# Second product of hidden groups 1 and 2 of the first MLP as seven block products, and all four W2 tiles of group 3 split behind them

## The chip, the cores and the metric

One Trainium2 chip, one of its cores. The kernel is a single program; its engines are TensorE (PE, with its weight loads shown apart as PEld), VectorE (DVE), ScalarE (ACT), GpSimd (POOL) and SyncE (SP), which issues nearly all DMAs. The metric is the device time of one execution in microseconds (us); the number given for a kernel is the median of several executions. A profile is one further execution, and its span runs from its first instruction to its last.

## What is computed

The reference, cut to what matters here (x has 2304 rows and 512 columns, each MLP has 2048 hidden features):

```python
kv  = np.einsum('bhsd,bhse->bhde', k, v)
out = np.einsum('bhsd,bhde->bhse', q, kv)
x   = out / rms(out) * g_norm          # regrouped to 2304 tokens x 512
h = x @ w_in                           # first MLP
x = softplus(h) @ w_out
h = x @ w_in2                          # second MLP
return leaky_relu(h, 0.01) @ w_out2
```

Each MLP is thus a first product (x @ w_in), a function of each element, and a second product (g @ w_out). The change touches second products of the first MLP alone.

## The kernel before, in words

**Numbers.** Every float32 operand of a matmul is held as two parts, a rounded one (ACT copies it, "high") and the rest (DVE subtracts, "low"). One product of two 128-deep tiles is therefore three matmuls: high by high, high by low, low by high.

**Tiles.** The hidden features of an MLP are cut into four groups of 512; groups 0 to 3 belong to the first MLP, 4 to 7 to the second. The 2304 tokens are cut into three pairs of two blocks of 384 (`BN`). One round of the main loop, a *pair* `t`, is one group and one pair of token blocks, so the MLPs are 24 pairs, three to a group. A pair has two steps `s` = 2t and 2t+1, each for half of the group's features (two tiles of 128). x, and what the second products add up to, lie in the tensor `xy`.

**First product, all groups.** Each step makes its 2 by 2 by 2 blocks with seven block products instead of eight (`product`, L819), from sums and differences of x blocks that are written to the DRAM scratch `xscr` once and loaded again for each pair (L802). `after` collects the results from PSUM (copies on ACT L1086, additions on DVE L1093) and applies the function.

**Second product, two ways.** In the plain way (`quarter`, L1135 for the first MLP, L1151 for the second) the eight combinations of feature half, token block and output half are made in four quarters of 24 matmuls, 96 matmuls of 384 columns for a pair; the results are added to `xy` by eight DVE additions (`to_xy`, L709). Its left operands are four W2 tiles that `split_w2` cuts into high and low (ACT L628, DVE L634). Its right operands are four hidden blocks that `parts` cuts into high and low (ACT L848, DVE L853). In the block way (`second`, L1046), used before in groups 5, 6 and 7, seven block products are made for a pair: `g_part` forms sums and differences of the hidden blocks (four DVE subtractions, L928) and splits seven of them (L848, L853); `w2_part` does the same with the W2 blocks once per group (four DVE operations L964, seven splits L978 and L981); `piece` i, j runs six matmuls, and `to_y` (L1025) adds what the PSUM bank holds to `xy` after each block product, fourteen additions for a pair. The second product of a pair is run one pair later, between the block products of the next first product.

**Weights.** W1 and W2 come as 64-bit numbers; `decode_w` loads a tile into one of two raw buffers (SP, L580 and L585) and builds float32 from it (ACT L594, DVE L600, L606, L612).

**Order.** The code records operations with their reads and writes; `Plan.run` then fixes the order on each engine ahead of time from a table of its own costs. On the chip every engine takes its list strictly in that order, and semaphores hold an instruction until what it reads is there and what it overwrites has been read.

**Buffers.** `rb` holds the split hidden blocks and W2 tiles, `rc` (once the attention is over) saved x blocks and decoded W2 tiles, `mf` hidden blocks and raw weights. The PSUM banks 0 to 3 serve the first product, 4 to 7 the second.

Of the kernel before, what the change touches and what calls it, by code (L numbers as in the profile page):

```python
# [131 lines left out]
def linear_attention_two_mlps(  # L132
# [154 lines left out]

    wx = [Reg("ra", at * KI, [2, 256]) for at in (18, 20)]

    gB = [Reg("rb", 6 * i * KI, [2, 2, BN]) for i in range(2)]  # L290
    gA = [Reg("rb", (12 + 6 * i) * KI, [2, 2, BN]) for i in range(3)]
    cB = Reg("mf", 20 * KI, [2, BN])
    cA = [Reg("mf", at * KI, [2, BN]) for at in (17, 4)]
    dram = ctx.enter_context(tc.tile_pool(name="dram", bufs=1, space=bass.MemoryType.DRAM))
    xscr = dram.tile([NTP * 7 + 1, P, 4 * BN], F32, name="xscr")

    SG = (NG + 1, NG + 2, NG + 3)
    cS = [Reg(n, at * KI, [2, BN]) for n, at in (("mf", 4), ("mf", 17), ("mf", 20), ("mf", 11), ("mf", 14), ("rc", 0))]
    gS = [Reg("rb", 6 * i * KI, [2, 2, BN]) for i in range(4)]
    wS = {j: Reg("rb", at * KI, [2, 2, 256]) for j, at in zip((1, 4, 5, 6, 3, 2, 0), (38, 42, 46, 50, 30, 34, 26))}  # L300
    fS = [[Reg("rc", (3 + 4 * u + 2 * m) * KI, [DM], I32) for m in range(2)] for u in range(2)]
    fT = Reg("rc", 11 * KI, [2, 256])

# [313 lines left out]
    def decode_pair(F, which, i):  # L617

        for m in range(2):
            decode_w(F + m, which, half[i][m])  # L620

    def split_w2(F, i):
        for m in range(2):
            d_, w_ = half[i][m], w2s[(F + m) % NW2]
            hk, lk = w_.keys(0, 4 * DM), w_.keys(4 * DM)
            op(
                {"A": t_a(DM)},
                lambda e, d_=d_, w_=w_: nc.scalar.activation(  # L628
                    w_[:, 0, :], d_.ap.bitcast(F32), AF.Copy
                ), d_.keys(), hk,  # L630
            )
            op(
                {"D": t_d(DM)},
                lambda e, d_=d_, w_=w_: ENG[e].tensor_tensor(  # L634
                    w_[:, 1, :], d_.ap.bitcast(F32), w_[:, 0, :].bitcast(F32), ALU.subtract
                ), d_.keys() + hk, lk,
            )

# [217 lines left out]

    FIRST = {(0, 0): 0, (1, 0): 1, (0, 1): 5, (1, 1): 6}

    def first_blocks():
# [15 lines left out]
            )  # L879

    def plain(s, k_):
        c, g_ = (cB, gB[s % 2]) if k_ else (cA[s % 2], gA[s % 3])
        w_ = wst[s % 2]
        for m in range(2):
            o = ps[2 + m][:, :BN]
            for j in range(2):

                e_, W_, part_ = xe[FIRST[j, k_]], *((wx[s], 0) if m + j == 0 else (w_, 2 * m + j - 1))

                def fn(e, j=j, o=o, e_=e_, W_=W_, part_=part_):  # L890
# [13 lines left out]
                op({"PE": 6 * t_mm[BN]}, fn, wk + e_.keys(), [("ps", 2 + m)])
            from_psum(c[:, m, :], o, BN, 2 + m, c.keys(4 * BN * m, 4 * BN * (m + 1)))
        act(s, lambda: c.ap, lambda: c.ap, 2 * BN, c.keys(), c.keys())
        parts(c, g_)

    def in_S(t):
        return t // NTP in SG  # L910

    S_pairs = [t for t in range(2 * NG * NTP) if in_S(t)]

    def block(t, u, k_):
        return cS[(4 * S_pairs.index(t) + 2 * u + k_) % len(cS)]

    def c_of(s):
        if in_S(s // 2):
            return block(s // 2, s % 2, 0), block(s // 2, s % 2, 1)
        return cA[s % 2], cB  # L920

    def g_part(t, i):
        b = {(u, k_): block(t, u, k_) for u in range(2) for k_ in range(2)}

        def minus(to, x, y):
            op(
                {"D": t_d(2 * BN)},
                lambda e: nc.vector.tensor_tensor(to.ap, x.ap, y.ap, ALU.subtract),  # L928
                x.keys() + y.keys(), to.keys(),
            )  # L930

        if i == 1:
            minus(b[0, 0], b[0, 1], b[0, 0])
        elif i == 2:
            minus(b[0, 0], b[1, 1], b[0, 0])
        elif i == 4:
            minus(b[0, 1], b[1, 1], b[0, 1])
        elif i == 6:
            minus(b[1, 0], b[1, 0], b[0, 0])
        src = b[((0, 0), (0, 0), (0, 0), (1, 1), (0, 1), (1, 0), (1, 0))[i]]  # L940
        parts(src, gS[(7 * S_pairs.index(t) + i) % len(gS)])

    def w2_decode(g, u):
        for m in range(2):
            decode_w(GF * g + 2 * u + m, 1, fS[u][m])

    def w2_part(i):


        def blk(a, u):  # L950
            at = (3 + 4 * u) * KI // 4
            ap = bufs["rc"][:, at:at + 2 * DM].rearrange("p (m f) -> p m f", m=2)
            return ap[:, :, a * 256:(a + 1) * 256]

# [12 lines left out]

        if i == 1:
            combine(4, 0, 1, ALU.add)
        elif i == 2:  # L970
            combine(0, 2, 0, ALU.subtract)
            combine(2, 4, 2, ALU.subtract)
        elif i == 3:
            combine(4, 3, 2, ALU.subtract)
        src, sk = r[(2, 4, 2, 4, 0, 3, 1)[i]]
        w_ = wS[PROD[i][2]]
        hk, lk = w_.keys(0, 2048), w_.keys(2048)
        op({"A": t_a(512)}, lambda e: nc.scalar.activation(w_[:, 0], src(), AF.Copy), sk, hk)  # L978
# [23 lines left out]
    def second(t):  # L1002
# [24 lines left out]
            )  # L1027

        def piece(i, j):
            w_ = wS[PROD[i][2]]  # L1030
            G_ = gS[(7 * S_pairs.index(t) + i) % len(gS)]
# [34 lines left out]
            if i + 4 < 7:  # L1066
                g_part(t, i + 4)
            elif in_S(t + 1):
                g_part(t + 1, i - 3)
            if t % NTP == NTP - 1 and g + 1 in SG:  # L1070
                w2_part(i)

        return [lambda i=i, j=j: piece(i, j) for i in range(7) for j in range(nj)]

    def after(s, i):
# [25 lines left out]
        elif i == 2:  # L1101
            copy(cB, 1, U, bu)
        elif i == 3:
            plus(cB, 1, V, bv)
        elif i == 4:
            plus(cB, 0, U, bu)
            act(s, lambda: cB.ap, lambda: cB.ap, 2 * BN, cB.keys(), cB.keys())
            if not in_S(s // 2):
                parts(cB, gB[s % 2])
        elif i == 5:  # L1110
            plus(cA_, 1, W, bw)
            act(s, lambda: cA_[:, 1, :], lambda: cA_[:, 1, :], BN, ck(cA_, 1), ck(cA_, 1))
        else:
            act(s, lambda: cA_[:, 0, :], lambda: U, BN, bu, ck(cA_, 0))
            if not in_S(s // 2):
                parts(cA_, gA[s % 3])

    y_no = [0]
    y_at = {}
# [1 line left out]
    def quarter(s, k_):  # L1121
# [2 lines left out]
        t, u = s // 2, s % 2  # L1124
        g, tp = t // NTP, t % NTP
        c0 = (2 * tp + k_) * BN
        G_ = gB[s % 2] if k_ else gA[s % 3]
        w_ = [w2s[(g * GF + 2 * u + m) % NW2] for m in range(2)]
        def features(j, m):
            y = ps[4 + j]  # L1130

            def fn(e):
                js = slice(j * P, (j + 1) * P)
# [107 lines left out]
    for s in range(2 * NT2 + 2):  # L1241
# [9 lines left out]
            rest = quarter(2 * t - 2, k_) + quarter(2 * t - 1, k_)  # L1251
        enters = t < NT2 and in_S(t) and not in_S(t - 1) and u == 1
        if enters:
            for i in range(2):
                g_part(t, i)
                w2_part(i)
        done = 0
        for i in range(7):
            if t == 0 and i in (0, 3):
# [23 lines left out]
        if enters:  # L1283
            g_part(t, 3)
            for i in range(2, 7):
                w2_part(i)
        if t >= NT2:
            continue
        F = (g + 1) * GF
        if g and no == 1 and g not in SG:  # L1290
            split_w2(g * GF + 2, 1)
        if g + 1 < 2 * NG:
            if no == (0 if g else 2) and g + 1 not in SG:
                decode_pair(F, 1, 0)
            if no == (1 if g else 2) and g + 1 not in SG:
                split_w2(F, 0)
            if no == 2:
                decode_pair(F, 0, 1)
# [3 lines left out]
                split_pair(1, 0)  # L1302
            if no == 5:
                split_pair(0, 1)
                if g + 1 not in SG:
                    decode_pair(F + 2, 1, 1)
            if g + 1 in SG and no >= 4:
                w2_decode(g + 1, no - 4)
    with tc.manual_schedule():

# [34 lines left out]
```

## Time and profile before

| | |
|---|---|
| median of 3 executions | 814.03 us (814.02 to 814.65) |
| the profiled execution | 812.92 us, of which 811.1 us are its span |
| PE busy | 798.1 us, 98% of the span, 5034 matmuls |
| DVE busy | 628.1 us, 77%, 1028 instructions |
| ACT busy | 442.7 us, 55%, 738 instructions |
| granted TensorE clock, mean | 1.00 of full speed |
| DMA | 192.47 MB, mean 237 GB/s |

Read it so: the matmuls of the two MLPs follow each other with hardly a gap, so that time is saved or lost where matmuls are left out, added or made to wait. DVE is the second busiest engine, but unevenly so: the share is a mean over stretches in which it is nearly full and others in which it is half empty.

### The profile page before, as it was taken

The page shows a single profiled execution, that of the slowest core. Times are in us where ns is not written, and L with a number is a line of the kernel's source. Part 1 is how long each engine was busy: PE and PEld are TensorE (multiplying, and loading weights), DVE is VectorE, ACT ScalarE, POOL GpSimd, SP SyncE. Part 2 cuts the span into 40 slices and gives each one's busy share as a digit, 9 for nine tenths or more (in the row PEclk, how much of TensorE's full clock was granted, in tenths as well). Part 3 has the DMA queues.
Part 4 walks back from the last instruction along what each step waited for, and adds up shares of the span by engine and source line. Part 5 has one row for each costly group of instructions (what it writes and reads, how often), then busy time and mean ns, then how long its engine had stood idle before and what let it go on. Part 6 is the DMA issues. An engine that isn't in the chain of part 4 may idle for free.

```text
span 811.1 us, 13058 instructions
## 1 busy us (share of the span) xinstructions
PE 798.1 (98%) x5034; PEld 784.9 (97%) x5034; DVE 628.1 (77%) x1028; ACT 442.7 (55%) x738; POOL 19.7 (2%) x35
## 2 busy tenths in 40 slices
PE   7899999999999999999999999999999999999997
PEld 6899999999999999999999988889999999999997
DVE  7998998955386744757489785968989999997776
ACT  6777877663354444444456655646446545554341
POOL 3420000000000000000000000000000000000000
PEclk9999999999999999999999999999999999999999
DMA  9990994685575863776867887956845755753913
GB/s 317 331 312 4 390 365 177 260 291 206 191 252 187 276 231 119 284 239 202 334 217 286 330 293 292 337 183 233 295 140 190 272 197 206 273 168 122 333 42 116
DMA packets 77293, 192.47 MB, mean 237 GB/s; under 512 B 11568, under 2 KB 50480, under 8 KB 77232
## 3 DMA queue, kind: packets, MB, share of 16 engines
q1 hardware_dynamic: 75344, 190.73, 66.0%
q10 hardware_dynamic: 1888, 0.92, 0.4%
q8 instruction: 39, 0.64, 0.3%
q14 instruction: 22, 0.18, 0.1%
HBM read 152.31 MB, written 39.32 MB: 236 GB/s over the span
## 4 chain that ended last, share of the span: by engine, by line
PE 96%; DVE 1%; ACT 1%; DMA 1%; issue 0%; SPq 0%; ACTq 0%
PE ps L819 41%; PE ps L1135 25%; PE ps L1046 17%; PE ps L1151 6%; PE ps L458 2%; PE ps L894 2%; PE ps L421 1%; PE ps L542 1%; DMA qr<-in_q_dram 1%; PE ps L413 1%; PE ps L464 0%; PE ps L424 0%; PE ps L554 0%; PE ps L417 0%; ACT xy L530 0%
## 5 line engine op out<-in xcount | busy, mean ns | idle before, releaser
L819 PE MATMUL ps<-ra 128*128 128x384 f32 x1932 | 387.4, 335 | 0.0
L819 PEld LDWEIGHTS ps<-ra 128*128 128x128 f32 x1932 | 334.9, 188 | 3.8
L1135 PE MATMUL ps<-rb 128*128 128x384 f32 x1152 | 226.8, 334 | 0.0
L1135 PEld LDWEIGHTS ps<-rb 128*128 128x128 f32 x1152 | 202.1, 188 | 0.0
L1046 PE MATMUL ps<-rb 128*128 128x256 f32 x1134 | 153.1, 281 | 0.0
L1046 PEld LDWEIGHTS ps<-rb 128*128 128x128 f32 x1134 | 148.7, 189 | 0.0
L1093 DVE TENSOR_TENSOR mf<-ps,mf 128x384 f32<-128x384 f32 x126 | 69.9, 555 | 89.1 <-PE ps L819 87.9
L848 ACT ACTIVATE rb<-mf 128x768 fp32r<-128x768 f32 x117 | 99.0, 846 | 63.7 <-PE ps L1046 46.5
L853 DVE TENSOR_TENSOR rb<-mf,rb 128x768 fp32r<-128x768 f32 x117 | 111.5, 953 | 15.3 <-ACT rb L848 15.1
L1086 ACT ACTIVATE mf<-ps 128x384 f32<-128x384 f32 x126 | 61.8, 491 | 92.7 <-PE ps L819 90.2
L1025 DVE TENSOR_TENSOR xy<-ps,xy 128x256 f32<-128x256 f32 (+1 forms) x129 | 69.7, 545 | 18.0 <-PE ps L1046 16.6
L834 ACT ACTIVATE mf<-mf 128x768 f32<-128x768 f32 (+1 forms) x48 | 33.5, 697 | 59.9 <-DVE mf L1093 59.8
L1151 PE MATMUL ps<-rb 128*128 128x512 f32 x216 | 56.8, 394 | 0.0
L709 DVE TENSOR_TENSOR xy<-ps,xy 128x384 f32<-128x384 f32 x72 | 40.0, 556 | 8.4 <-PE ps L1135 8.0
L1151 PEld LDWEIGHTS ps<-rb 128*128 128x128 f32 x216 | 39.9, 188 | 5.7
L840 ACT ACTIVATE mf<-mf 128x384 f32<-128x384 f32 (+1 forms) x42 | 27.6, 657 | 23.6 <-DVE mf L1093 23.5
L704 ACT ACTIVATE xy<-ps 128x384 f32<-128x384 f32 (+1 forms) x35 | 18.7, 535 | 13.4 <-PE ps L1135 9.8
L606 DVE SCALAR_TENSOR_TENSOR sqr<-mf,sqr 128x512 int32<-128x512 int32 x35 | 24.0, 685 | 0.3
L928 DVE TENSOR_TENSOR mf<-mf 128x768 f32<-128x768 f32 x24 | 22.9, 955 | 0.9 <-ACT mf L840 0.3
L600 DVE TENSOR_SCALAR sqr<-mf 128x512 int32<-128x512 int32 x28 | 11.9, 424 | 15.1 <-ACT mf L594 14.1
L675 DVE TENSOR_TENSOR ra<-mf,ra 128x768 fp32r<-128x768 f32 (+1 forms) x18 | 19.5, 1085 | 1.5 <-ACT ra L671 1.5
L606 DVE SCALAR_TENSOR_TENSOR sqr<-lf,sqr 128x512 int32<-128x512 int32 x29 | 20.0, 689 | 0.6
(112 smaller groups left out, 709.4 us busy)
## 6 DMA issues: line engine op xcount, KB each, us to landing
ra<-xscr SPq DMA_DIRECT2D x131, 768.0 KB, 6.0
xscr<-ra SPq DMA_DIRECT2D x30, 768.0 KB, 6.2
mf<-in_moe_w_in_dram SPq DMA_DIRECT2D x18, 512.0 KB, 6.0
xscr<-rc SPq DMA_DIRECT2D x12, 768.0 KB, 3.4
mf<-in_moe_w_out_dram SPq DMA_DIRECT2D x17, 512.0 KB, 4.6
lf<-in_moe_w_out_dram SPq DMA_DIRECT2D x15, 512.0 KB, 3.5
lf<-in_moe_w_in_dram SPq DMA_DIRECT2D x14, 512.0 KB, 5.2
qa<-in_q_dram SPq DMA_DIRECT2D x16, 256.0 KB, 5.2
```

Of the source, the lines that this page charges most:

```text
L606: lambda e: nc.vector.scalar_tensor_tensor(t_, r[:, :, 0], 29, t_, ALU.logical_shift_right, ALU.bitwise_or), rk + tk, tk,
L709: {"D": t_d(n)}, lambda e: nc.vector.tensor_tensor(dst, src, dst, ALU.add),
L819: nc.tensor.matmul(o, w_[:, a, c:c + P], e_[:, b, kk, :], start=(not on and kk == 0 and n == 0), stop=(kk == 1 and n == 2), skip_group_che ...
L834: {"A": t_a(n)}, lambda e: nc.scalar.activation(dst(), src(), AF.Softplus),
L848: {"A": t_a(n)}, lambda e: nc.scalar.activation(g[:, 0, :, :], c.ap, AF.Copy),
L853: lambda e: nc.vector.tensor_tensor(g[:, 1, :, :], c.ap, g[:, 0, :, :].bitcast(F32), ALU.subtract),
L1025: {"D": t_d(n)}, lambda e: nc.vector.tensor_tensor(dst, src, dst, ALU.add),
L1046: nc.tensor.matmul(y[:, 256 * (j % 2):256 * (j % 2 + 1)], G_[:, a, m, js], w_[:, b, m, :], **flags)
L1086: {"A": t_a(BN)}, lambda e: nc.scalar.activation(c[:, m, :], src, AF.Copy),
L1093: lambda e: nc.vector.tensor_tensor(c[:, m, :], src, c[:, m, :], ALU.add),
L1135: nc.tensor.matmul(y[:, :BN], w_[m][:, a, js], G_[:, b, m, :], start=(u == 0 and m == 0 and i == 0), stop=(u == 1 and m == 1 and i == 2),)
L1151: nc.tensor.matmul(y, G_[:, a, m, js], w_[m][:, b, :], start=(u == 0 and m == 0 and i == 0), stop=(u == 1 and m == 1 and i == 2),)
```

## The change

It does four things.

1. Groups 1 and 2 join groups 5, 6 and 7 in `SG`, so that their second product runs as seven block products, in the form for the first MLP (`w_` as left operand, 384 columns, two pieces to a block product).
2. The split hidden blocks no longer have fixed places for plain and block pairs (`gA`, `gB`, `gS`): five places `gR` are handed out and given back (`g_new`, `g_read`), the fifth being closed while a block stretch of the first MLP holds W2 blocks over it (`g_held`). The W2 blocks get a second set of places for groups 1 and 2 (`wS[0]`).
3. Group 3, plain, now follows a block group. All four of its W2 tiles are decoded into the buffers of the block way and split (`split_tile`) in the last pair of group 2 behind the block products 2 to 5, and the hidden blocks of its first pair are split there too (`late`) instead of in `after`.
4. The W2 tiles of group 1 are decoded in the first step of group 1 (`g == 1 and no == 0`), since `rc` holds x blocks until then.

Cut to its core:

```diff
-    gB = [Reg("rb", 6 * i * KI, [2, 2, BN]) for i in range(2)]
-    gA = [Reg("rb", (12 + 6 * i) * KI, [2, 2, BN]) for i in range(3)]
+    gR = [Reg("rb", 6 * i * KI, [2, 2, BN]) for i in range(5)]
...
-    SG = (NG + 1, NG + 2, NG + 3)
+    SG = (1, 2, NG + 1, NG + 2, NG + 3)
...
-    gS = [Reg("rb", 6 * i * KI, [2, 2, BN]) for i in range(4)]
-    wS = {j: Reg("rb", at * KI, [2, 2, 256]) for j, at in zip((1, 4, 5, 6, 3, 2, 0), (38, 42, 46, 50, 30, 34, 26))}
+    wS = [
+        {j: Reg("rb", at * KI, [2, 2, 256]) for j, at in zip((1, 4, 5, 6, 3, 2, 0), ats)}
+        for ats in ((46, 50, 30, 34, 38, 42, 26), (38, 42, 46, 50, 30, 34, 26))
+    ]
...
+    def g_new(key, reads):
+        at = next(i for i in g_free if not (g_held[0] and i == len(gR) - 1))
+        g_free.remove(at)
+        g_live[key] = [at, reads]
+        return gR[at]
...
+    def g_read(key):
+        g_live[key][1] -= 1
+        if not g_live[key][1]:
+            g_free.append(g_live.pop(key)[0])
...
+    def leaves(t):
+        return 0 < t < 2 * NG * NTP and in_S(t - 1) and not in_S(t)
+
-    S_pairs = [t for t in range(2 * NG * NTP) if in_S(t)]
+    S_pairs = [t for t in range(2 * NG * NTP) if in_S(t) or leaves(t)]
...
             elif in_S(t + 1):
                 g_part(t + 1, i - 3)
+            elif leaves(t + 1):
+                if i == 6:
+                    g_held[0] = False
+                s, k_ = divmod(i - 3, 2)
+                late(2 * (t + 1) + s, 1 - k_)
+            if leaves(t + 1) and 2 <= i <= 5:
+                split_tile(fS[(i - 2) // 2][i % 2], w2s[(GF * (g + 1) + i - 2) % NW2])
             if t % NTP == NTP - 1 and g + 1 in SG:
-                w2_part(i)
+                w2_part(g + 1, i)
...
-            if not in_S(s // 2):
-                parts(cB, gB[s % 2])
+            if s // 2 not in S_pairs:
+                parts(cB, g_new((s, 1), reads(s)))
...
+        if g == 1 and no == 0:
+            for u_ in range(2):
+                w2_decode(g, u_)
+        by_pairs = g + 1 not in SG and g not in SG
         if g + 1 < 2 * NG:
-            if no == (0 if g else 2) and g + 1 not in SG:
+            if no == (0 if g else 2) and by_pairs:
                 decode_pair(F, 1, 0)
...
-            if g + 1 in SG and no >= 4:
+            if g and not by_pairs and no >= 4:
                 w2_decode(g + 1, no - 4)
```

What stands in the engines' lists then, in two places. The names: `ps_83` to `ps_90` are the PSUM banks 0 to 7 in that order, `ra` holds x blocks and W1, `rb` split hidden blocks and W2, and a row with x6 is six instructions in a row.

**PE, second pair of group 1.** Before, two or four sets of three plain matmuls (L1135) stand between two block products of the first product (L819):

```order
L819 MATMUL ps_83<-ra 128x384 x6
L1135 MATMUL ps_88<-rb 128x384 x3
L1135 MATMUL ps_89<-rb 128x384 x3
L819 MATMUL ps_85<-ra 128x384 x6
L1135 MATMUL ps_89<-rb 128x384 x3
L1135 MATMUL ps_90<-rb 128x384 x3
L1135 MATMUL ps_87<-rb 128x384 x3
L1135 MATMUL ps_90<-rb 128x384 x3
L819 MATMUL ps_83<-ra 128x384 x6
```

After, one piece of six matmuls (L1077) stands between two block products (now L821):

```order
L821 MATMUL ps_83<-ra 128x384 x6
L1077 MATMUL ps_87<-rb 128x384 x6
L821 MATMUL ps_86<-ra 128x384 x6
L1077 MATMUL ps_88<-rb 128x384 x6
L821 MATMUL ps_83<-ra 128x384 x6
L1077 MATMUL ps_89<-rb 128x384 x6
L821 MATMUL ps_84<-ra 128x384 x6
L1077 MATMUL ps_90<-rb 128x384 x6
L821 MATMUL ps_85<-ra 128x384 x6
```

What moved: before, a bank takes four sets of three matmuls and is then read once, and sixteen sets share a step with seven block products of the first; after, a bank is read behind each piece of six, the two pieces of a block product use one couple of banks (`ps_87` and `ps_88`, or `ps_89` and `ps_90`), and seven pieces share a step with seven block products.

**DVE, the first pair of group 1, where the block way begins.** Before, the places between the additions of `after` (L1093) hold weight decoding (L600, L606, L612), the splits of two W2 tiles (L634) and of hidden blocks (L853):

```order
L853 TENSOR_TENSOR rb<-mf,rb 128x768
L1093 TENSOR_TENSOR mf<-ps_85,mf 128x384
L634 TENSOR_TENSOR rb<-lf,rb 128x512
L1093 TENSOR_TENSOR mf<-ps_84,mf 128x384
L634 TENSOR_TENSOR rb<-lf,rb 128x512
L600 TENSOR_SCALAR sqr<-lf 128x512
L606 SCALAR_TENSOR_TENSOR sqr<-mf,sqr 128x512
L1093 TENSOR_TENSOR mf<-ps_86,mf 128x384
L853 TENSOR_TENSOR rb<-mf,rb 128x768
L612 SCALAR_TENSOR_TENSOR lf<-lf,sqr 128x512
```

After, the last W2 tile of group 1 is decoded (L601, L607, L613), and the sums of W2 blocks (L989), their splits (L1006) and the differences of hidden blocks (L952) follow:

```order
L613 SCALAR_TENSOR_TENSOR rc<-rc,sqr 128x512
L952 TENSOR_TENSOR mf<-mf 128x768
L989 TENSOR_TENSOR rc<-rc 128x512
L989 TENSOR_TENSOR rc<-rc 128x2x256
L855 TENSOR_TENSOR rb<-mf,rb 128x768
L1006 TENSOR_TENSOR rb<-rc,rb 128x512
L1126 TENSOR_TENSOR mf<-ps_85,mf 128x384
L989 TENSOR_TENSOR rc<-rc 128x2x256
L989 TENSOR_TENSOR rc<-rc 128x512
L1006 TENSOR_TENSOR rb<-rc,rb 128x512 x2
L1126 TENSOR_TENSOR mf<-ps_84,mf 128x384
L1006 TENSOR_TENSOR rb<-rc,rb 128x512
...
L1050 TENSOR_TENSOR xy<-ps_87,xy 128x384
L855 TENSOR_TENSOR rb<-mf,rb 128x768
L1006 TENSOR_TENSOR rb<-rc,rb 128x512
L1050 TENSOR_TENSOR xy<-ps_88,xy 128x384
```

What moved: W2 sums and splits and hidden differences stand ahead of the first piece; the last split of a W2 block stands behind the first two additions of `to_y` (L1050), whose blocks it does not feed.

Counted over the whole program, PE has 72 matmuls of 384 columns fewer (576 plain ones fewer, 504 in pieces more). DVE has 18 more splits of hidden blocks, 24 more differences of them, 8 more W2 sums, 14 more W2 block splits, 8 fewer splits of plain W2 tiles, 84 more additions of `to_y` against 48 fewer of `to_xy`, and 9 copies of the first group's results that stood on ACT.

## Rows read from the trace of the kernel before

**Rows 1.** Stretches: busy time and instructions (x) of each engine, in us.

```profile
core 0: us, PE busy (x) PEld busy (x) DVE busy (x) ACT busy (x) POOL busy (x), PEclk, DMA share, GB/s
85.90:148.30 62.40, 62.40 (x361) 62.40 (x361) 58.28 (x85) 48.03 (x81) 0.00 (x0) 1.00 0.80 315
148.30:179.50 31.20, 31.20 (x181) 31.20 (x181) 21.88 (x36) 19.38 (x36) 0.00 (x0) 1.00 0.71 249
179.50:366.70 187.20, 187.20 (x1081) 187.20 (x1081) 111.84 (x186) 82.27 (x131) 0.00 (x0) 1.00 0.64 223
559.48:737.00 177.52, 177.52 (x1263) 177.52 (x1262) 165.79 (x267) 93.67 (x146) 0.00 (x0) 1.00 0.60 217
707.41:737.00 29.59, 29.59 (x213) 29.59 (x212) 29.06 (x47) 17.23 (x27) 0.00 (x0) 1.00 0.53 187
```

**Rows 2.** The chain that ended last: start, length, engine, line, instructions.

```profile
155.57 2.08 PE ps L1135 x12
...
451.97 2.08 PE ps L1135 x12
...
559.48 1.43 PE ps L1046 x12
...
737.00 1.43 PE ps L1046 x12
```

**Rows 3.** Groups by line and form: count, busy us, mean ns, idle before.

```profile
L853 DVE TENSOR_TENSOR rb<-mf,rb 128x768 fp32r<-128x768 f32 x117 | 111.5, 953 | 15.3 <-ACT rb L848 15.1
...
L1025 DVE TENSOR_TENSOR xy<-ps,xy 128x512 f32<-128x512 f32 x60 | 41.2, 687 | 7.5 <-PE ps L1046 6.9
L709 DVE TENSOR_TENSOR xy<-ps,xy 128x384 f32<-128x384 f32 x72 | 40.0, 556 | 8.4 <-PE ps L1135 8.0
...
L1025 DVE TENSOR_TENSOR xy<-ps,xy 128x256 f32<-128x256 f32 x69 | 29.0, 422 | 10.5 <-PE ps L1046 9.7
...
L928 DVE TENSOR_TENSOR mf<-mf 128x768 f32<-128x768 f32 x24 | 22.9, 955 | 0.9 <-ACT mf L840 0.3
```

**Rows 4.** DVE in order of time, groups 5 and 6: start, length, line, form.

```profile
580.22 0.68 DVE L612 SCALAR_TENSOR_TENSOR rc<-rc,sqr 128x512 int32<-128x512 int32 x1
580.82 0.95 DVE L928 TENSOR_TENSOR mf<-mf 128x768 f32<-128x768 f32 x1
581.69 0.42 DVE L1025 TENSOR_TENSOR xy<-ps,xy 128x256 f32<-128x256 f32 x1
582.02 0.55 DVE L1093 TENSOR_TENSOR mf<-ps,mf 128x384 f32<-128x384 f32 x1
582.49 0.95 DVE L928 TENSOR_TENSOR rc<-mf,rc 128x768 f32<-128x768 f32 x1
583.35 0.95 DVE L853 TENSOR_TENSOR rb<-mf,rb 128x768 fp32r<-128x768 f32 x1
584.22 1.01 DVE L1025 TENSOR_TENSOR xy<-ps,xy 128x512 f32<-128x512 f32 x2
```

**Rows 5.** Waits from 556 to 740 us: total, times, longest us.

```profile
DVE xy L1025 <- PE ps L1046: 7.1, 20, 1.1
...
DVE rb L853 <- ACT rb L848: 3.1, 9, 0.5
...
DVE rb L981 <- ACT rb L978: 1.5, 2, 1.2
...
DVE mf L1093 <- PE ps L819: 0.4, 1, 0.4
```

**Rows 6.** Waits from 140 to 340 us: total, times, longest us.

```profile
DVE sqr L600 <- ACT mf L594: 5.8, 6, 2.1
...
ACT mf L594 <- DMA lf<-in_moe_w_in_dram: 4.2, 2, 2.2
```

**Rows 7.** Waits of SyncE's DMA queue from 140 to 340 us.

```profile
SPq L802 <- PE ps L819: 114.0, 42, 17.3
SPq L580 <- DVE sqr L606: 31.6, 8, 9.1
```

More of the change, by code (lines that the diff above doesn't have):

```diff
@@ L620, in decode_pair, with split_tile @@
             decode_w(F + m, which, half[i][m])
+    def split_tile(d_, w_):
+        hk, lk = w_.keys(0, 4 * DM), w_.keys(4 * DM)
+        op(
+            {"A": t_a(DM)},
+            lambda e: nc.scalar.activation(w_[:, 0, :], d_.ap.bitcast(F32), AF.Copy),
+            d_.keys(), hk,
+        )
+        op(
+            {"D": t_d(DM)},
+            lambda e: nc.vector.tensor_tensor(
+                w_[:, 1, :], d_.ap.bitcast(F32), w_[:, 0, :].bitcast(F32), ALU.subtract
+            ), d_.keys() + hk, lk,
+        )
     def split_w2(F, i):
         for m in range(2):
[L624 to L637, printed above, removed]
+            split_tile(half[i][m], w2s[(F + m) % NW2])
     def part(r, j, n=1):
@@ L857, in parts, with g_reg, reads @@
         )
+    g_free, g_live, g_held = list(range(len(gR))), {}, [False]
+    def g_new(key, reads):
[3 more added lines that the diff above has]
+        return gR[at]
+    def g_reg(key):
+        return gR[g_live[key][0]]
+    def g_read(key):
+        g_live[key][1] -= 1
+        if not g_live[key][1]:
+            g_free.append(g_live.pop(key)[0])
+    def reads(s):
+        return 8 if s // 2 // NTP < NG else 2 * BN // P
     FIRST = {(0, 0): 0, (1, 0): 1, (0, 1): 5, (1, 1): 6}
@@ L881, in plain @@
     def plain(s, k_):
-        c, g_ = (cB, gB[s % 2]) if k_ else (cA[s % 2], gA[s % 3])
+        c = cB if k_ else cA[s % 2]
         w_ = wst[s % 2]
@@ L906, in plain @@
         act(s, lambda: c.ap, lambda: c.ap, 2 * BN, c.keys(), c.keys())
-        parts(c, g_)
+        parts(c, g_new((s, k_), reads(s)))
     def in_S(t):
         return t // NTP in SG
-    S_pairs = [t for t in range(2 * NG * NTP) if in_S(t)]
+    def leaves(t):
+        return 0 < t < 2 * NG * NTP and in_S(t - 1) and not in_S(t)
+    S_pairs = [t for t in range(2 * NG * NTP) if in_S(t) or leaves(t)]
     def block(t, u, k_):
@@ L917, in c_of @@
     def c_of(s):
-        if in_S(s // 2):
+        if s // 2 in S_pairs:
             return block(s // 2, s % 2, 0), block(s // 2, s % 2, 1)
@@ L940, in g_part @@
         src = b[((0, 0), (0, 0), (0, 0), (1, 1), (0, 1), (1, 0), (1, 0))[i]]
-        parts(src, gS[(7 * S_pairs.index(t) + i) % len(gS)])
+        g = t // NTP
+        parts(src, g_new((t, "S", i), 2 if g < NG else BN // P))
     def w2_decode(g, u):
@@ L945, in w2_decode, with w2_part @@
             decode_w(GF * g + 2 * u + m, 1, fS[u][m])
-    def w2_part(i):
+    def w2_part(g, i):
         def blk(a, u):
@@ L975, in w2_part @@
         src, sk = r[(2, 4, 2, 4, 0, 3, 1)[i]]
-        w_ = wS[PROD[i][2]]
+        w_ = wS[g // NG][PROD[i][2]]
         hk, lk = w_.keys(0, 2048), w_.keys(2048)
@@ L1029, in piece @@
         def piece(i, j):
-            w_ = wS[PROD[i][2]]
-            G_ = gS[(7 * S_pairs.index(t) + i) % len(gS)]
+            w_ = wS[g // NG][PROD[i][2]]
+            G_ = g_reg((t, "S", i))
+            g_read((t, "S", i))
             bank = (6 if i in (1, 3, 5) else 4) + (j // 2 if tokens else j)
@@ L1114, in after, with late @@
             act(s, lambda: cA_[:, 0, :], lambda: U, BN, bu, ck(cA_, 0))
-            if not in_S(s // 2):
-                parts(cA_, gA[s % 3])
+            if s // 2 not in S_pairs:
+                parts(cA_, g_new((s, 0), reads(s)))
+    def late(s, k_):
+        parts(c_of(s)[k_], g_new((s, k_), reads(s)))
     y_no = [0]
@@ L1126, in quarter @@
         c0 = (2 * tp + k_) * BN
-        G_ = gB[s % 2] if k_ else gA[s % 3]
         w_ = [w2s[(g * GF + 2 * u + m) % NW2] for m in range(2)]
@@ L1130, in features @@
             y = ps[4 + j]
+            G_ = g_reg((s, k_))
+            g_read((s, k_))
             def fn(e):
@@ L1146, in tokens @@
             y = ps[yb]
+            G_ = g_reg((s, k_))
+            g_read((s, k_))
             def fn(e):
@@ L1253, in linear_attention_two_mlps @@
         if enters:
+            g_held[0] = True
             for i in range(2):
                 g_part(t, i)
-                w2_part(i)
+                w2_part(t // NTP, i)
         done = 0
@@ L1285, in linear_attention_two_mlps @@
             for i in range(2, 7):
-                w2_part(i)
+                w2_part(t // NTP, i)
         if t >= NT2:
@@ L1289, in linear_attention_two_mlps @@
         F = (g + 1) * GF
-        if g and no == 1 and g not in SG:
+        if g and no == 1 and g not in SG and g - 1 not in SG:
             split_w2(g * GF + 2, 1)
+        if g == 1 and no == 0:
+            for u_ in range(2):
+                w2_decode(g, u_)
+        by_pairs = g + 1 not in SG and g not in SG
         if g + 1 < 2 * NG:
-            if no == (0 if g else 2) and g + 1 not in SG:
+            if no == (0 if g else 2) and by_pairs:
                 decode_pair(F, 1, 0)
-            if no == (1 if g else 2) and g + 1 not in SG:
+            if no == (1 if g else 2) and by_pairs:
                 split_w2(F, 0)
@@ L1304, in linear_attention_two_mlps @@
                 split_pair(0, 1)
-                if g + 1 not in SG:
+                if by_pairs:
                     decode_pair(F + 2, 1, 1)
-            if g + 1 in SG and no >= 4:
+            if g and not by_pairs and no >= 4:
                 w2_decode(g + 1, no - 4)
```

## The prediction

> **What bounds the kernel now.** I read the chain of work that ended last first, since it says which engine sets the end. Through both MLPs it is PE alone, in an even beat: in the plain part of the first MLP the run of twelve L1135 matmuls that ends a step stands at 155.57 us and, 19 steps later, at 451.97 us [rows 2]. That is 296.40 / 19 = 15.60 us a step, for 42 matmuls of the first product and 48 of the second, all of 384 columns: 15.60 / 90 = 0.1733 us each. In the block part the same mark stands at 559.48 and 737.00 us, six pairs later: 29.59 us a pair, again without a hitch [rows 2].
>
> Next I read the stretches, because the mean DVE share (77%) hides what the change meets. PE is busy from end to end of each of them [rows 1]. DVE is not: the six pairs from 179.5 to 366.7 us (steps 8 to 19, in which PE runs the plain second products of groups 1 and 2) hold 111.84 us of DVE work in 187.20 us, 60%. The six pairs from 559.48 to 737.00 us, block products of groups 5 and 6, hold 165.79 us in 177.52 us, 93%; in the last of them it is 29.06 of 29.59 us, 98% [rows 1]. So the trace already holds a stretch run the way that groups 1 and 2 are to run, and in it DVE is nearly full and PE doesn't slow down.
>
> **The change part by part.** *Matmuls removed.* A plain pair has 96 matmuls of the second product, a block pair 7 x 2 x 6 = 84, of the same 384 columns. Six pairs lose 12 each: 72 matmuls x 0.1733 us = **12.5 us** off the chain, and a step shrinks to 84 x 0.1733 = 14.56 us. The pieces have the operand forms of the plain matmuls (W2 tile on the left, 384 columns of `rb`), so I give them the same pace. The Trainium skill (TensorE: Matmul & The Clock Gate, Back-to-back issue gap) gives N / 2.4 + 2.5 ns for a matmul by itself, 162.5 ns here; by that the gain would be 11.7 us. The rows, which are of this stream, decide.
>
> *DVE work added.* In each of the six pairs there are four differences and three splits of 768 elements more, and fourteen additions of 384 columns to `xy` instead of eight. What one costs when DVE doesn't wait is the distance between starts, not the length: 0.87 us for 768 elements, 0.60 for 512, 0.47 for 384, 0.33 for 256, each some 0.085 us less than its length, since the next starts before the last has ended [rows 4]. A pair gains 7 x 0.87 + 6 x 0.47 = 8.9 us, six pairs 53.5. The W2 blocks of a group are 4 sums and 7 splits of 512 elements, 11 x 0.60 = 6.6 us; those of group 2 fall into the six pairs, those of group 1 ahead of them. Some two plain W2 splits leave, 1.2 us.
>
> *Does it fit?* From above: 111.84 + 53.5 + 6.6 - 1.2 = 170.7 us in 6 x 29.12 = 174.7 us, 98%; that is too much, for a busy time read in a half-empty stretch counts each instruction's overlapping tail. From below: a block pair of the first MLP has the same DVE list as one of the second (6 additions in `after`, 4 differences, 7 splits, 14 additions to `xy`) but for the form of the last, 14 of 384 columns (2 x 0.556 = 1.11 us) in place of 7 of 512 and 7 of 256 (0.687 + 0.422 = 1.11 us) [rows 3]. So I take 165.8 us of groups 5 and 6, less one set of W2 blocks (6.6, since group 3 is plain), plus the four splits of group 3 (2.4): 161.6 us, 92.5%. I take this one, being like for like; both ends lie at or below the 98% at which PE already ran on without a wait [rows 1]. I cost DVE's work at nothing.
>
> *What hides it, and what if the cover goes.* A pair of banks is taken up again after two pieces in the other pair, with a product between each: some six runs of six matmuls, 6 x 1.04 = 6.2 us from the end of a piece to the next use of its bank. An addition of 0.56 us may come over 5 us late before PE waits. Should DVE fall further behind than that, the additions to `xy` hold the pieces, the splits hold the next products' operands, and PE takes DVE's time.
>
> *Entry.* The pair from 148.3 to 179.5 us has 21.88 us of DVE work [rows 1]. It gets the W2 blocks of group 1 (6.6), two differences (1.7), and loses four plain splits (2.4): 27.8 of 31.2 us. It follows two pairs with 58.28 of 62.40 us [rows 1], to which nine copies of 384 columns come (4.2 us, from ACT), so DVE enters with something to catch up on. The last W2 blocks stand in DVE's list behind the first additions of `to_y`, and feed the sixth and seventh block product, ten pieces on. Queued behind a late decode on DVE are the sums and splits for the first piece; nothing in the trace shows this chain at this place. Its price lies between nothing and the longest links of such a chain here, 2.1 us (DVE for ACT) and 2.2 us (ACT for a weight load) [rows 6]. I take nothing, as in the entry into group 5, after which the beat starts at once.
>
> *Leaving.* In the last pair of group 2 four W2 splits and four block splits move forward; they are needed in the step after. Same bounds, nothing taken.
>
> *ACT and DMA.* ACT is busy 53% in groups 5 and 6 [rows 1] and gets no more here. Bytes don't change. All 42 loads of x blocks in the stretch wait for PE, not PE for them [rows 7]. Weight loads wait in SP's list for DVE to free a raw buffer, 31.6 us in eight waits, at most 9.1 [rows 7]; with a fuller DVE these grow, and x loads stand behind them. A step to spare (14.6 us) covers that.
>
> *Sum.* The profiled execution is 812.92 us, 811.1 of it span: 12.5 less is 800.4 and 798.6. It lies 1.1 us below the median of the runs; against that median, 814.03 - 12.5 = **801.5 us**, a gain of 1.5%.
>
> **The rivals.**
> 1. *A wait once at entry or leaving.* For: a new chain of load, decode, sum, split at a place where DVE comes in full. Against: ten pieces of slack. At 2.2 us for one link it gives 803.7, at both links (4.3 us) 805.8.
> 2. *DVE instructions don't overlap once it is full.* Then 260 instructions (267 in groups 5 and 6, less 7) cost 0.085 us more each: 161.6 + 22.1 = 183.7 us against 174.7, 9.0 us lost: 810.5. The Trainium skill speaks for it (VectorE: DVE Perf Modes, The DRAIN you can't avoid): the next operation waits until the pipe of the last has emptied. The trace disagrees: 0.87 us between starts of 0.95 us instructions [rows 4]; and groups 5 and 6 would have needed 165.8 + 267 x 0.085 = 188.5 us in a stretch that took 177.5.
> 3. *Slower: DVE becomes the bound and its waits add up too.* DVE takes its list in order; in groups 5 and 6 it stood idle for others 7.1 + 3.1 + 1.5 + 0.4 = 12.1 us [rows 5]. If those waits do not shrink as DVE falls behind, and instructions don't overlap, the six pairs take 183.7 + 12.1 = 195.8 us: 21.1 more than forecast, 822.6. It decides from 31.2 us of DVE time a pair, where the gain is gone. Against it stands that PE in groups 5 and 6 never waited for DVE, with the same list.
> 4. *It does nothing.* Excluded: 72 matmuls are gone from PE's list, and PE is the chain.
>
> **How the numbers follow.** The forecast, 800.4 to 802.6, has a chance of 0.87; rival 1 0.08; rival 2 0.02; rival 3 0.02; and 0.01 for a tail of the program that the planner ordered otherwise. The range runs from 800.4 (all runs like the profiled one) to 803.8 (one link of rival 1), which leaves out rival 1's upper half and rivals 2 and 3. A change of 0.2% (1.6 us) is about what a measurement of this kernel can tell from none: faster 0.96 (forecast, rivals 1 and 2), same 0.01, slower 0.03.
>
> **What the profile after would show.** Right: from about 180 us a beat of 29.1 us a pair over six pairs, 12.5 us off every later mark; DVE at 92 to 98% there; no wait of PE for DVE or ACT after the attention. Rival 1 would show as one PE wait near 180 or 355 us, on a split of W2 or of a hidden block. Rival 2 as pairs of some 30.6 us with starts on DVE 0.95 us apart, rival 3 as pairs above 31.2 us with PE waiting on the additions to `xy`. The prediction is wrong if the pairs are not even.

## The result

The changed kernel takes 801.01 us (median of 4 executions, 800.57 to 801.79) against 814.02 us before; the ratio is 0.9842, 95% interval 0.9825 to 0.9859. Forecast were 801.5 us, within 800.4 to 803.8. The profiled execution took 800.57 us, its span is 798.5 us; before they were 812.92 and 811.1.

The chain that ended last, in the changed kernel from 140 to 400 us (start, length, engine, line, instructions; L1172 is now the line of the plain matmuls):

```profile
155.37 2.08 PE ps L1172 x12
...
170.97 2.08 PE ps L1172 x12
...
361.29 2.08 PE ps L1172 x12
376.89 2.08 PE ps L1172 x12
```

These are the marks of [rows 2]: a run of twelve plain matmuls where a step ends. They are missing from 171 to 361 us, where no plain second product runs any more. Before, the mark at 155.57 us comes again 14 steps of 15.60 us later, at 373.97:

```profile
373.97 2.08 PE ps L1135 x12
```

Now the one at 155.37 has its counterpart at 361.29. The interval shrank from 218.40 to 205.92 us, by 12.48 us, and 72 x 0.1733 is 12.48. Nothing was lost at entry, within, or at leaving.

Stretches of the changed kernel: the pair of entry, the six block pairs one by one, and all six (busy us and instructions of each engine, granted clock, DMA):

```profile
core 0: us, PE busy (x) PEld busy (x) DVE busy (x) ACT busy (x) POOL busy (x), PEclk, DMA share, GB/s
148.30:179.50 31.20, 31.20 (x182) 31.20 (x181) 28.25 (x45) 19.01 (x35) 0.00 (x0) 1.00 0.69 255
179.50:208.62 29.12, 29.12 (x170) 29.12 (x169) 27.26 (x46) 16.06 (x26) 0.00 (x0) 1.00 0.68 246
208.62:237.74 29.12, 29.12 (x170) 29.12 (x169) 27.10 (x45) 16.01 (x25) 0.00 (x0) 1.00 0.70 249
237.74:266.86 29.12, 29.12 (x170) 29.12 (x169) 28.69 (x48) 17.05 (x28) 0.00 (x0) 1.00 0.59 209
...
325.10:354.22 29.12, 29.12 (x170) 29.12 (x169) 28.18 (x50) 18.84 (x32) 0.00 (x0) 1.00 0.67 247
179.50:354.22 174.72, 174.72 (x1010) 174.72 (x1009) 165.67 (x275) 97.72 (x155) 0.00 (x0) 1.00 0.65 237
```

Where [rows 1] had DVE busy 111.84 of 187.20 us it is now busy 165.67 of 174.72, 95%, in the third of the pairs 28.69 of 29.12, 98.5%. PE is busy throughout. What DVE still waits for there (total, times, longest us):

```profile
DVE xy L1050 <- PE ps L1077: 5.0, 19, 0.5
DVE mf L1126 <- PE ps L821: 1.1, 3, 0.5
DVE rb L855 <- ACT rb L850: 0.8, 3, 0.3
DVE rc L1126 <- PE ps L821: 0.2, 1, 0.2
```

DVE waits for PE and ACT, for half a microsecond at most. PE waits for nobody after the attention. The groups by line that are new or grew (count, busy us, mean ns, idle before):

```profile
L1077 PE MATMUL ps<-rb 128*128 128x384 f32 x504 | 100.8, 334 | 0.0
...
L1050 DVE TENSOR_TENSOR xy<-ps,xy 128x384 f32<-128x384 f32 x84 | 46.5, 554 | 5.9 <-PE ps L1077 5.0
```

The 504 matmuls of the pieces never waited, and the 84 additions have the length that [rows 3] gives for the plain ones.

### The profile page after: what moved, and what is told of

Read it like the earlier page. It is cut to its first block, busy times and chain, and to the rows that moved or that the text cites. A ratio compares the mean times of both kernels' runs of the same rounds, so it can differ in the third digit from the quotient of the medians.

```text
span 798.5 us, 13018 instructions
## 1 busy us (share of the span) xinstructions
PE 787.5 (99%) x4962; PEld 774.9 (97%) x4962; DVE 688.2 (86%) x1129; ACT 453.3 (57%) x753; POOL 18.2 (2%) x35
## 4 chain that ended last, share of the span: by engine, by line
PE 97%; ACT 1%; DMA 1%; DVE 1%; SPq 0%; issue 0%; POOL 0%; ACTq 0%; POOLq 0%
PE ps L821 42%; PE ps L1072 17%; PE ps L1172 13%; PE ps L1077 11%; PE ps L1190 6%; PE ps L459 2%; PE ps L915 2%; PE ps L422 2%; PE ps L414 1%; PE ps L543 1%; DMA qa<-in_q_dram 1%; PE ps L465 0%; PE ps L425 0%; PE ps L555 0%; ACT xy L531 0%
## 5 line engine op out<-in xcount | busy, mean ns | idle before, releaser
L821 PE MATMUL ps<-ra 128*128 128x384 f32 x1932 | 387.4, 335 | 0.0
L821 PEld LDWEIGHTS ps<-ra 128*128 128x128 f32 x1932 | 334.9, 188 | 3.8
L850 ACT ACTIVATE rb<-mf 128x768 fp32r<-128x768 f32 x131 | 110.8, 846 | 91.9 <-PE ps L1072 43.9
L1072 PEld LDWEIGHTS ps<-rb 128*128 128x128 f32 x1134 | 148.7, 189 | 0.0
L855 DVE TENSOR_TENSOR rb<-mf,rb 128x768 fp32r<-128x768 f32 x131 | 124.6, 953 | 16.0 <-ACT rb L850 15.5
L1050 DVE TENSOR_TENSOR xy<-ps,xy 128x512 f32<-128x512 f32 (+2 forms) x213 | 116.3, 549 | 23.2 <-PE ps L1072 16.1
L1172 PE MATMUL ps<-rb 128*128 128x384 f32 x576 | 113.7, 334 | 0.0
L1172 PEld LDWEIGHTS ps<-rb 128*128 128x128 f32 x576 | 101.1, 188 | 0.0
L1077 PE MATMUL ps<-rb 128*128 128x384 f32 x504 | 100.8, 334 | 0.0
L1126 DVE TENSOR_TENSOR mf<-ps,mf 128x384 f32<-128x384 f32 x118 | 65.4, 554 | 36.6 <-PE ps L821 35.1
L1077 PEld LDWEIGHTS ps<-rb 128*128 128x128 f32 x504 | 88.5, 188 | 0.0
L1190 PEld LDWEIGHTS ps<-rb 128*128 128x128 f32 x216 | 39.9, 188 | 5.7
L952 DVE TENSOR_TENSOR mf<-mf 128x768 f32<-128x768 f32 x40 | 38.1, 953 | 0.8 <-ACT mf L842 0.3
L1006 DVE TENSOR_TENSOR rb<-rc,rb 128x512 fp32r<-128x512 f32 x35 | 23.8, 685 | 2.0 <-ACT rb L1003 2.0
L1003 ACT ACTIVATE rb<-rc 128x512 fp32r<-128x512 f32 x35 | 21.5, 626 | 5.7 <-PE ps L1190 2.4
L607 DVE SCALAR_TENSOR_TENSOR sqr<-mf,sqr 128x512 int32<-128x512 int32 x35 | 24.0, 685 | 0.3
L706 ACT ACTIVATE xy<-ps 128x512 f32<-128x512 f32 (+1 forms) x26 | 14.2, 548 | 14.6 <-PE ps L1172 11.6
```

The source lines that it names most:

```text
L821: nc.tensor.matmul(o, w_[:, a, c:c + P], e_[:, b, kk, :], start=(not on and kk == 0 and n == 0), stop=(kk == 1 and n == 2), skip_group_che ...
L850: {"A": t_a(n)}, lambda e: nc.scalar.activation(g[:, 0, :, :], c.ap, AF.Copy),
L855: lambda e: nc.vector.tensor_tensor(g[:, 1, :, :], c.ap, g[:, 0, :, :].bitcast(F32), ALU.subtract),
L1050: {"D": t_d(n)}, lambda e: nc.vector.tensor_tensor(dst, src, dst, ALU.add),
L1072: nc.tensor.matmul(y[:, 256 * (j % 2):256 * (j % 2 + 1)], G_[:, a, m, js], w_[:, b, m, :], **flags)
L1077: nc.tensor.matmul(y[:, :BN], w_[:, a, m, js], G_[:, b, m, :], **flags)
```

## The experiments

All times are medians; the kernel before ran beside each lot (814.29 us in the first lot of four, 813.63 in the second). Profiled executions differ by up to 2.3 us before the first block pair (the mark that stands at 108.57 us in the changed kernel stands at 107.78 us in one run and at 110.07 us in another, and neither run's edit touches anything ahead of it); so for single microseconds I also compare the interval between the marks that stand at 170.97 and 361.29 us in the changed kernel, 190.32 us.

**Only the count of matmuls.** The kernel before, less 12 matmuls a plain pair, in `quarter`:

```diff
                 for i, (a, b) in enumerate(((0, 0), (0, 1), (1, 0))):
+                    if g in (1, 2) and i == 1 and m == 0 and j < 3:
+                        continue
                     nc.tensor.matmul(
```

> The kernel before, with 12 matmuls of each plain pair of groups 1 and 2 left out (the high-by-low matmul of the first tile of a half, for three of four output tiles), 72 in all; everything else stands as before, so the sums for groups 1 and 2 lack those terms. Theory A (the gain is the count of matmuls and nothing else): 814.0 - 72 x 0.1733 = 801.5 us, within 0.2% of the changed kernel. Rival B (the added DVE work, entry or leaving cost something in the changed kernel that even beats hide): this kernel is faster than the changed one by more than 1.6 us. Rival C (the block form helps in another way, through fewer bank readings or another order): this kernel is slower than the changed one by more than 1.6 us.

Measured: 801.09 us, ratio 0.9844 (0.9828 to 0.986). The marks:

```profile
171.77 2.08 PE ps L1137 x12
...
362.09 2.08 PE ps L1137 x12
```

190.32 us, to the hundredth what the changed kernel shows. The six pairs in this kernel (columns as above):

```profile
179.50:354.22 174.72, 174.72 (x1010) 174.72 (x1009) 110.36 (x185) 82.01 (x131) 0.00 (x0) 1.00 0.66 237
```

DVE has 110.36 us of work in them instead of 165.67. So 55 us of added DVE work cost nothing, and the block form brings nothing beyond its fewer matmuls. Theory A holds, B and C fall.

**How much more DVE work fits.** In the changed kernel some of the seven low splits of a block pair of groups 1 and 2 are issued twice, without telling the planner, so that every list stays in its order (one, three or all of seven):

```diff
+        def lo(e):
+            for _ in range(times):
+                nc.vector.tensor_tensor(
+                    g[:, 1, :, :], c.ap, g[:, 0, :, :].bitcast(F32), ALU.subtract
+                )
...
-        parts(src, g_new((t, "S", i), 2 if g < NG else BN // P))
+        parts(src, g_new((t, "S", i), 2 if g < NG else BN // P), 2 if g < NG and i in (1, 3, 5) else 1)
```

> The changed kernel, with one of the seven low splits of each block pair of groups 1 and 2 issued twice (same result, same order of everything else): 6 more DVE instructions of 768 elements. Theory A (DVE is hidden, 165.7 of 174.7 us busy in the six pairs): 6 x 0.87 = 5.2 us more gives 170.9, still less than PE's 174.7, so 801.0 us, same within 0.2%. Rival 2 (DVE is already the bound, or nearly, one instruction after another): 6 x 0.95 = 5.7 us on the time, 806.7 us.

> As the run with one, with three of seven low splits issued twice: 18 more DVE instructions. Theory A: 165.7 + 18 x 0.87 = 181.3 us of DVE work against 174.7 us of PE, so PE begins to wait; by the excess 6.6 us, 807.6 us; less if the busy time still holds overlapping tails (down to 803). Rival 2: 18 x 0.95 = 17.1 us, 818.1 us.

> As the run with one, with all seven low splits issued twice: 42 more DVE instructions. Theory A: 165.7 + 42 x 0.87 = 202.2 us against 174.7, DVE is the bound, 27.5 us more, 828.5 us; from the run with three to this one each further instruction costs its distance between starts, 24 x 0.87 = 20.9 us. Rival 2: 42 x 0.95 = 39.9 us, 840.9 us.

| more DVE instructions | time, us | ratio to before (95%) | above the changed kernel |
|---|---|---|---|
| 6 | 801.40 | 0.9845 (0.983 to 0.986) | 0.4 |
| 18 | 803.81 | 0.9877 (0.9859 to 0.9895) | 2.8 |
| 42 | 827.09 | 1.0162 (1.0145 to 1.0179) | 26.1 |

With six the interval between the marks (171.58 and 361.90 us) is 190.32 us again: nothing lost. With 18 (170.86 and 363.85 us) it is 2.67 us longer, with 42 DVE is the bound and the gain is more than gone. I had put 18 repeats at 807.6 us, or down to 803 should the busy time hold overlapping tails; 803.81 us lies near that lower end, so DVE had more room than the sum of busy times left it. Who PE waited for, with 18 and with 42 (after the attention):

```profile
PE ps L821 <- DVE mf L1129: 1.1, 2, 0.8
PE ps L821 <- DVE rc L1129: 0.5, 1, 0.5
```

```profile
PE ps L821 <- DVE mf L1129: 9.5, 6, 2.3
PE ps L821 <- ACT rc L1122: 3.9, 2, 2.2
PE ps L821 <- DVE rc L1129: 2.2, 3, 1.0
PE ps L1080 <- DVE xy L1053: 1.4, 2, 0.7
PE ps L821 <- ACT mf L1122: 0.5, 2, 0.3
```

L1129 is the addition of `after`, L1053 that of `to_y`. What gives first here is the first product (L821), not the pieces.

From 18 to 42 each further instruction cost 23.3 / 24 = 0.97 us, more than the 0.87 I expected and near the 0.95 of rival 2. The order in time on DVE, with 42, shows why:

```profile
229.12 1.95 DVE L852 TENSOR_TENSOR rb<-mf,rb 128x768 fp32r<-128x768 f32 x2
230.99 0.55 DVE L1053 TENSOR_TENSOR xy<-ps,xy 128x384 f32<-128x384 f32 x1
231.46 0.95 DVE L677 TENSOR_TENSOR ra<-lf,ra 128x768 fp32r<-128x768 f32 x1
```

Two repeats take 1.95 us, about 0.99 from the first start to the second: the repeat starts only after the one in front has ended. It writes what that one writes, which I take for the reason; no run tests the reason by itself. The next instruction follows 0.88 us after the second started, before its end. The dose was thus dearer than I priced it, while the other instructions overlap as [rows 4] had it; rival 2 stays out. That 42 repeats came out at 827.09 us, near the 828.5 expected, is in part luck: the room was larger than I had reckoned (3.8 us at 18 repeats), and each repeat beyond was dearer.

**Half of it, entering and leaving all the same.** The block way for group 1 alone, group 2 plain:

```diff
-    SG = (1, 2, NG + 1, NG + 2, NG + 3)
+    SG = (1, NG + 1, NG + 2, NG + 3)
...
-                split_tile(fS[(i - 2) // 2][i % 2], w2s[(GF * (g + 1) + i - 2) % NW2])
+                n = (2, 3, 0, 1)[i - 2]
+                split_tile(fS[n // 2][n % 2], w2s[(GF * (g + 1) + n) % NW2])
```

> The changed kernel with the block way for group 1 alone in the first MLP (group 2 plain again, its four W2 tiles split behind the block products of group 1's last pair, in the order 2, 3, 0, 1). Theory A (the gain is the count of matmuls): 36 fewer than before instead of 72, so 801.0 + 36 x 0.1733 = 807.3 us, half of the gain, though entering and leaving are both still paid. Rival 1 (entering or leaving costs something once): above that by the cost, 808.5 us or more.

Measured: 806.80 us, ratio 0.9911 (0.9891 to 0.9932). That is 5.8 us above the changed kernel for 36 matmuls more (6.2 us), and no PE wait after the attention. By the marks (170.98 and 445.54 us, in the changed kernel 170.97 and 439.29) it is 6.24 us, the price of 36 matmuls to the hundredth. The gain goes by the count; no fixed price is left over.

**One group more.** `SG` with 1, 2 and 3. In this kernel x parts of the second MLP are staged in `rc` over the decoded W2 tiles of group 4 before these are split, so part of group 4's second product is made from other numbers; the amount of work is not changed by that.

> The changed kernel with the block way for group 3 as well (group 4, plain, follows it). 36 matmuls fewer still: 6.2 us. Theory A with DVE's capacity as its limit: the six steps in which group 3's second product runs hold 73.6 us of DVE work in 93.6 us in the changed kernel, because the x parts of the second MLP are made there; 3 x 8.9 us for differences, splits and additions and 6.6 us for W2 blocks, less 2.4 for plain splits, give 104.5 us against 87.4 us of PE, 17 us too much. So DVE is the bound there, the 6.2 us are lost again and more: 801 to 812 us, I say 806. Theory that only the count of matmuls matters, wherever: 794.8 us.

Measured: 807.06 us, ratio 0.9911 (0.9894 to 0.9928): 36 matmuls fewer, 6 us slower than the changed kernel. The last pair of group 3's second product, and who PE waited for:

```profile
412.50:441.60 29.10, 22.98 (x107) 21.37 (x106) 29.10 (x45) 18.49 (x27) 0.00 (x0) 0.85 0.68 260
```

```profile
PE ps L1077 <- DVE xy L1050: 6.4, 5, 2.5
```

DVE is busy without a gap, PE 79% of the time. The sum of DVE work against PE time, 104.5 against 87.4 us, had the place right and the size too large: it gives 17 us too much, and the run lost 12.3 us against the 794.8 us that the count of matmuls alone gives. In this run the pieces wait, and the first product does not. The block way pays up to the point at which DVE is full, and group 3, with the x parts of the second MLP in it, is past it.

**Differences also to GpSimd.** As the last, with the differences of `g_part` and `x_part` open to GpSimd (the edit of `g_part`; `x_part` gets the same):

```diff
-                {"D": t_d(2 * BN)},
-                lambda e: nc.vector.tensor_tensor(to.ap, x.ap, y.ap, ALU.subtract),
+                {"D": t_d(2 * BN), "P": t_p(2 * BN)},
+                lambda e: ENG[e].tensor_tensor(to.ap, x.ap, y.ap, ALU.subtract),
```

> As the run with groups 1, 2 and 3, with the differences of hidden blocks and of x blocks open to GpSimd as well as DVE (the list put 33 or so of them on GpSimd). If DVE's capacity is what limits group 3, taking differences of 0.87 us each off it, some 10 around group 3, gives back about 8 us: 798 us, unless the two engines hinder each other at SBUF or GpSimd is too slow for the next split; then no faster than without, 806 us.

Measured: 809.29 us, ratio 0.9947 (0.9931 to 0.9963), 2.2 us slower than without GpSimd. I had expected 798 us, or 806 if the two engines hinder each other; it is slower than both. GpSimd and DVE in order of time, in two views:

```profile
417.83 1.90 POOL L769 TENSOR_TENSOR mf<-xy 128x768 f32<-128x768 f32 x1 [3.83 <-DVE xy L1050]
420.69 2.14 POOL L952 TENSOR_TENSOR mf<-rc,mf 128x768 f32<-128x768 f32 x1 [0.96 <-DVE rb L855]
```

```profile
417.94 2.60 DVE L855 TENSOR_TENSOR rb<-mf,rb 128x768 fp32r<-128x768 f32 x1
420.47 0.68 DVE L607 SCALAR_TENSOR_TENSOR sqr<-lf,sqr 128x512 int32<-128x512 int32 x1
421.07 0.54 DVE L1050 TENSOR_TENSOR xy<-ps,xy 128x384 f32<-128x384 f32 x1
421.54 2.11 DVE L734 TENSOR_TENSOR ra<-xy,ra 128x768 fp32r<-128x768 f32 x1
```

The two splits of DVE that begin while GpSimd is at work take 2.60 and 2.11 us instead of 0.95, and end 0.8 us after GpSimd's instruction does; the addition with an input in PSUM (L1050) keeps its 0.54 us. In this run 56 differences stand on GpSimd, more than the 33 or so that I had counted. DVE has 1119 instructions instead of 1175 and is busy as long as in the run before, 717.5 us against 717.1: what was moved to GpSimd cost DVE all that it saved. The Trainium skill says so in kind (Perfetto Trace Analysis, Optimizing Scalar/DVE Operations: GpSimd and DVE share a read port of SBUF, so that offloading between the two may not help); the trace agrees, with these lengths.

**Entry made heavier.** Each low split of group 1's W2 blocks issued twice:

```diff
+        def lo(e):
+            for _ in range(2 if g == 1 else 1):
+                nc.vector.tensor_tensor(w_[:, 1], src(), w_[:, 0].bitcast(F32), ALU.subtract)
```

> The changed kernel with each of the seven low splits of group 1's W2 blocks issued twice (same result): 7 x 0.6 to 0.7 = 4.2 to 4.9 us more DVE work in the entry. Theory A (entry has slack: 28.25 of 31.20 us busy in the pair ahead of the first block pair, and an addition may come some 5 us late): 801.0 us, same within 0.2%. Rival 1 (entry is at its limit): 2 us more where DVE's free 2.95 us are used up, 803; 4.9 us more if nothing is free, 806.

Measured: 802.96 us, ratio 0.9858 (0.9837 to 0.9879), 1.95 us above the changed kernel. The profile has this (the two marks, then a repeat on DVE and a wait of PE at entry, then the waits of PE's weight loads, which begin earlier than the matmuls'):

```profile
172.47 2.08 PE ps L1171 x12
...
363.89 2.08 PE ps L1171 x12
```

```profile
178.73 1.41 DVE L1006 TENSOR_TENSOR rb<-rc,rb 128x512 fp32r<-128x512 f32 x2
...
178.87 1.32 PE L821 MATMUL ps<-ra 128*128 128x384 f32 x6 [0.16 <-DVE mf L1125]
```

```profile
PEld ps L821 <- DVE rc L1125: 0.7, 1, 0.7
PEld ps L821 <- DVE mf L1125: 0.5, 1, 0.5
```

The interval is 191.42 us, 1.10 us longer than in the changed kernel. (This execution took 803.23 us; 1.50 us of its distance to the profiled one of the changed kernel stand at the first mark, and stood there at 95 us already.) A repeat adds 1.41 - 0.685 = 0.73 us, seven 5.1 us, so four fifths were hidden and one fifth was not. I had expected nothing, 801.0 us: the entry has less to spare than I thought. The median is that of rival 1 as written down, 803 us once DVE's free 2.95 us are used up; by the interval, 1.10 us, less was lost. Again PE waits for an addition of `after` (L1125).

## Why the prediction was right, point by point

**The chain and the price of a matmul.** Right: 12.48 us measured, 12.5 forecast. The matmuls of the pieces keep the pace of 0.1733 us, and the whole interval confirms it: a gain of 11.7 us would have left the counterpart mark at 362.07 us and not at 361.29.

**DVE fits.** Right. Of the two sums, 161.6 and 170.7 us, I took the lower; the profile has 165.67. The measured value lies between. The higher one takes in the overlapping ends of instructions in a half-empty stretch, as I wrote; the lower one left work out: the six pairs hold 275 DVE instructions, not the 260 that I took over from groups 5 and 6. The lists were not alike in weight decoding, with 53 instructions here (L601, L607, L613) against 35 there. That the work is hidden was shown by the plain kernel with 72 matmuls fewer, not only by the even beat.

**Rivals 2 and 3.** They fall. Rival 3's own condition, a DVE pair of more than 31.2 us, was produced by 42 repeats, and gave 827 us. In that run DVE has hardly a gap, and the view of waits lists none of DVE from 180 to 380 us:

```profile
179.50:354.22 174.72, 159.04 (x876) 154.09 (x875) 172.67 (x269) 79.03 (x130) 0.00 (x0) 0.98 0.59 205
```

So one half of the mechanism is real, DVE as the bound, and the changed kernel is some 6 to 18 instructions away from where it begins; the other half, DVE's own waits on top, did not come about.

**Rival 1.** Nothing was paid at entry or leaving. The room to spare at entry is smaller than I argued, though. The pair ahead of the first block pair was sized well (28.25 us of DVE work, forecast 27.8). The two pairs before it were not: I had DVE enter behind them with something to catch up on, more than their 58.28 us, and they hold less now:

```profile
85.90:148.30 62.40, 62.40 (x362) 62.40 (x361) 55.91 (x83) 43.69 (x71) 0.00 (x0) 1.00 0.76 299
```

**The step that was mis-sized: how late DVE may come.** I counted 6.2 us from a piece to the next use of its pair of banks. Inside a pair the way is that long or longer. But `piece` gives the last block product of a pair and the first of the next the same two banks, so there only three runs of six matmuls lie between two uses of one bank, 3 x 1.04 = 3.1 us. The two pieces that waited with 42 repeats stand there; counted in the trace, each is the second piece of a pair:

```profile
215.30 1.33 PE L1080 MATMUL ps<-rb 128*128 128x384 f32 x6 [0.70 <-DVE xy L1053]
...
248.77 1.33 PE L1080 MATMUL ps<-rb 128*128 128x384 f32 x6 [0.72 <-DVE xy L1053]
```

The additions of `after` stand in the same list, and the PE rows of the change show an equally short way for them, in every step: the first product's bank `ps_83` is used, then come a piece, a block product in another bank and a piece, and `ps_83` is used again, 3.1 us. The first waits with 18 repeats and with the heavier entry were for such additions; the trace does not name the bank, but in `after` only this addition has so short a way. The forecast did not suffer, because DVE never fell that far behind.

**What stays open.** Leaving was not made heavier by itself; that it costs nothing rests on the interval between the marks, which spans it.

## What to carry to other kernels

When one engine's list is the whole time, first count its instructions at the pace of the trace; then look for a stretch of the same kernel that already runs the new way, and read there whether the engine that takes on the work keeps up. Sum the work of that second engine stretch by stretch, by distances between starts: the same change gained 12.5 us in groups 1 and 2 and lost 6 us in group 3, because of what else was made there. The first waits come where the way back to a buffer is shortest, among all the buffers that the engine's list serves. Once the engine has more work than time, another wait may come first, as that of the pieces did in group 3; no run here shows what decides that.

## What the runs showed of the hardware that I had not expected

- A DVE instruction that repeats the one right in front of it, to the same place, loses the overlap: 1.41 us for two of 512 elements (0.685 each, with some 0.03 between), where free ones start 0.60 us apart [rows 4].
- A DVE instruction of 768 elements with both inputs in SBUF that begins during a GpSimd difference ends only 0.8 us after that does: 2.60 us instead of 0.95 in the longest of the rows shown. In the run with GpSimd this holds for 25 of the 26 that began so.
- When DVE held PE up in group 3, TensorE's granted clock fell with it. The stretches of that run (columns as above):

```profile
415.00:420.00 5.00, 5.00 (x31) 5.00 (x30) 5.00 (x9) 2.52 (x6) 0.00 (x0) 1.00 0.96 383
420.00:425.00 5.00, 3.10 (x17) 2.46 (x15) 5.00 (x9) 3.59 (x6) 0.00 (x0) 1.00 0.57 236
425.00:430.00 5.00, 3.56 (x11) 3.42 (x12) 5.00 (x8) 0.97 (x2) 0.00 (x0) 0.58 0.90 311
430.00:435.00 5.00, 4.69 (x22) 4.18 (x21) 5.00 (x10) 2.89 (x5) 0.00 (x0) 0.74 0.71 252
435.00:440.00 5.00, 2.52 (x13) 2.21 (x12) 5.00 (x8) 4.84 (x6) 0.00 (x0) 0.94 0.30 120
440.00:445.00 5.00, 4.68 (x20) 4.17 (x20) 5.00 (x9) 4.24 (x7) 0.00 (x0) 0.71 0.62 208
445.00:450.00 5.00, 5.00 (x31) 5.00 (x30) 5.00 (x9) 3.74 (x7) 0.00 (x0) 1.00 0.99 302
```

PE is full to 420 us, then busy 3.10 of 5.00 us, and in the next stretch the mean granted clock is 0.58 of full speed, most of the time at the lower of its two levels (1.2 of 2.4 GHz): 11 matmuls in 3.56 us of busy time, where 31 go into 5.00 us at full clock. That this cost time in this run is not shown: DVE is busy through all these stretches. In the run with GpSimd such matmuls stand in the chain that ended last, 12 of them in 3.85 us, 0.32 us each instead of 0.1733:

```profile
435.47 1.92 PE ps L1077 x6
437.39 1.93 PE ps L821 x6
```

There a wait of PE is paid twice. In the changed kernel the clock stays at 1.00 in each of the six pairs.
